# Chunked attention and a feed-forward layer on one core: smaller warming products, a held-back weight load and a new order of the first steps

## The chip, the cores and the metric

The kernel runs on one core of one Trainium2 chip. The metric is the device time of one execution in microseconds (us). The engines are TensorE (PE, matrix products; its weight loads are listed apart as PEld), VectorE (DVE), ScalarE (ACT), GpSimd (POOL) and SyncE (SP), whose queue issues the DMA transfers here.

## The reference

```python
chunk, scale = 64, 1 / np.sqrt(64)                   # q, k, v: [8, 8, 576, 64] float32
q_c, k_c, v_c = (a.reshape(8, 8, 9, 64, 64) for a in (q, k, v))
scores = scale * np.matmul(q_c, k_c.transpose(0, 1, 2, 4, 3))
scores = scores - np.max(scores, axis=-1, keepdims=True)
attn = np.exp(scores)
attn = attn / (np.sum(attn, axis=-1, keepdims=True) + 1e-09)
out = np.matmul(attn, v_c)
x = out.transpose(0, 2, 1, 3).reshape(4608, 512)
h = x @ w_in                                         # [512, 2048] float64
g = h * (1 / (1 + np.exp(-1.702 * h)))
return (g @ w_out).astype(np.float32)                # [2048, 512] float64
```

## The kernel before

The 4608 tokens are worked in nine blocks of 512. For each block the attention gives x, transposed, as a high and a low part (`x_h`, `x_l`); the first layer makes 16 groups of 128 hidden columns (`h_j`: three products of 512 columns for each of four slices of 128 dimensions, high by high, low by high, high by low); the gate gives `g_h` and `g_l`; the second layer adds them up in four PSUM tiles `po0` to `po3` (`o_j_t`). The weights arrive as float64 words. For group j (or for its halves j_0, the column part of w_in, and j_1, the row part of w_out, with j = 0 and 1), `raw` loads them, `wsc` and `wlow` (ACT), `wshift` and `wj` (DVE) turn the words into float32, and `wh` (ACT) and `w` (DVE) split that into two parts.

The change works on the start, in which nothing can be multiplied yet. The attention of the first block is done by `plan_first(u)` in four groups u = 0 to 3, each of two heads with 512 tokens. The steps of a group, with their engines: `q_u`, `k_u`, `v_u` (SP: loads, 256 KB each, into tiles `first_a` and `first_b`), `tqp_u` and `tkp_u` (PE: transposes by products with the identity; for u = 0 and 2 as 16 products of 64 by 64 each, L541, for u = 1 and 3 as 8 of 128 by 64 each, L549), `tq_u` and `tk_u` (ACT, for u = 1 `tk_u` on DVE: copies out of PSUM, L561 to L570), `s_u` (PE: 16 score products, L579), `m_u` and `sm_u` (DVE: maximum L584, subtraction L588), `ex_u` (ACT: exponential, L591), `z_u` (DVE: sum L595, plus 1e-9 L596, reciprocal L598), `n_u` (POOL: multiplication, L601), `ep_u` (PE: four transposes, L606), `et_u` (ACT: copy, L613), `xp_u` (PE: 16 products with v, L628), `xh_u` (ACT, L636) and `xl_u` (DVE, L640). A float32 product that isn't a transpose by the hardware's own mode is two loads and two products in the trace.

Before the first transposes, PE multiplies the identity by itself (`keep_warm`, L1720); nothing reads the result. A tile of the constant 1e-9 (`eps`) is set at the start.

What stands when is set by a table: `ORDER` is one string with the names of all 2754 steps, and `Plan.emit` runs the steps in that order, so that each engine gets its instructions in the order of the names; an engine works strictly in its own order and waits by semaphores. A DMA semaphore can be used again only when its last transfer has landed, so that SP has at most eight loads under way.

```python
plan.add(DMA, (n, 1.5, 384), at - 5.5, load, need=slot_users(j), make=e("raw"), take=[tag])
plan.add(PE, 3.4, -1000, lambda: keep_warm(ps_o, "po3", WARM), make="warm")
```

Of the kernel before, what the change touches and what calls it, by code (L numbers as in the profile page):

```python
# [237 lines left out]
def tile_chunk_attention_ffn(  # L238
# [20 lines left out]
    NTL = NT // P  # L259
    NB = NTL // TB  # L260
    BT = TB * P
    SCALE = 1.0 / float(D) ** 0.5
    NPE = 6
    NTMP = 3
    WARM = 7
    FILL = ()
    NH = 2
    RANKS = (-1.0, 9.0, 14.0, 20.0, 21.5, 31.0, 35.0, 37.5, 45.5, 52.0, 62.0, 70.0, 76.0, 82.5, 92.5, 100.0)
    K_ACT = (0, 2, 3)
    LOW_DVE = ()  # L270
    LEAD = 25
# [1514 lines left out]
```

## Time and profile before

| | |
|---|---|
| median of 3 runs | 813.99 us (812.33 to 816.24) |
| profiled execution, own time | 814.22 us |
| its span in the profile | 812.4 us |
| PE busy in the span | 803.3 us (99%) |
| DVE, ACT, POOL busy | 595.0, 380.3, 90.0 us |
| first stretch of PE without gaps begins | about 25.5 us |

The span runs from the first instruction to the last one; the execution's own time is 1.8 us longer. A PE that is shown as busy is not PE at its peak, since products are pipelined and their ends are modelled. Times below are counted from the start of the span.

### The profile page before, as it was taken

How to read it: one execution, taken by the hardware profiler on the slowest of the kernel's cores; microseconds unless marked ns; L12 is line 12 of the kernel's file. 1: busy time of each engine (PE TensorE's matmuls, PEld its weight loads, DVE VectorE, ACT ScalarE, POOL GpSimd, SP SyncE). 2: the span in 40 equal slices, each digit the busy share in tenths (PEclk: the TensorE clock that was granted, in tenths of full speed). 3: DMA queues.
4: the chain of work that ended last, by engine and by line, in shares of the span. 5: the costliest groups of instructions: out<-in, count | busy, mean ns of one | idle time of the engine just before them, and what ended most of it. 6: DMA issues, size and time to landing. Idle time of an engine off the chain costs nothing.

```text
span 812.4 us, 15467 instructions
## 1 busy us (share of the span) xinstructions
PE 803.3 (99%) x5934; PEld 666.6 (82%) x5934; DVE 595.0 (73%) x900; ACT 380.3 (47%) x610; POOL 90.0 (11%) x83
## 2 busy tenths in 40 slices
PE   7999999999999999999999999999999999999998
PEld 6788888888888888888888888888888888888887
DVE  4888974646567979886787888876878545659965
ACT  5998934334445546413345451523554512338450
POOL 1100004030045651000000010000001000000000
PEclk9999999999999999999999999999999999999999
DMA  9995646642366677667664538676533046766433
GB/s 266 301 349 127 160 94 182 166 97 52 66 186 169 172 198 215 179 184 216 180 159 130 133 80 217 178 215 192 156 118 105 0 128 193 230 202 220 134 100 105
DMA packets 240106, 133.17 MB, mean 164 GB/s; under 512 B 179104, under 2 KB 207776, under 8 KB 240032
## 3 DMA queue, kind: packets, MB, share of 16 engines
q1 hardware_dynamic: 240032, 132.18, 58.0%
q8 instruction: 47, 0.77, 0.4%
q14 instruction: 27, 0.22, 0.1%
HBM read 97.52 MB, written 32.51 MB: 160 GB/s over the span
## 4 chain that ended last, share of the span: by engine, by line
PE 97%; DMA 1%; ACT 0%; issue 0%; DVE 0%; SPq 0%; DVEq 0%
PE po L1643 13%; PE po L1645 13%; PE po L1644 13%; PE hp L867 9%; PE hp L869 9%; PE hp L868 9%; PE hp L1607 5%; PE hp L1609 5%; PE hp L1608 5%; PE acc_A L1133 3%; PE acc_B L1133 3%; PE s L1387 2%; PE x L1461 2%; PE acc_A L1126 2%; PE acc_B L1126 1%; DMA first_a<-in_k_dram 1%
## 5 line engine op out<-in xcount | busy, mean ns | idle before, releaser
L1643 PE MATMUL po<-w,g_l 128*128 128x512 f32 x448 | 176.4, 394 | 0.0
L1645 PE MATMUL po<-w,g_h 128*128 128x512 f32 x448 | 174.5, 390 | 0.0
L1644 PE MATMUL po<-w,g_h 128*128 128x512 f32 x448 | 174.5, 389 | 0.0
L1643 PEld LDWEIGHTS po<-w,g_l 128*128 128x128 f32 x448 | 84.1, 188 | 18.4 <-DVE g_l L918 0.4
L1645 PEld LDWEIGHTS po<-w,g_h 128*128 128x128 f32 x448 | 84.1, 188 | 17.6
L1644 PEld LDWEIGHTS po<-w,g_h 128*128 128x128 f32 x448 | 84.1, 188 | 16.9
L867 PE MATMUL hp<-w,w 128*128 128x512 f32 x224 | 87.5, 390 | 0.1
L869 PE MATMUL hp<-w,w 128*128 128x512 f32 x224 | 87.2, 389 | 0.0
L868 PE MATMUL hp<-w,w 128*128 128x512 f32 x224 | 87.2, 389 | 0.0
L1436 DVE STREAM_TRANSPOSE eT<-e 32x512 f32<-32x512 f32 x120 | 84.2, 702 | 3.1 <-POOL e L1417 1.2
L1417 POOL TENSOR_TENSOR e<-e,r 128x1024 f32<-128x1024 f32 x16 | 31.5, 1968 | 436.4 <-DVE r L1414 338.9
L1607 PE MATMUL hp<-x_l,w 128*128 128x512 f32 x184 | 72.1, 392 | 0.0
L1608 PE MATMUL hp<-x_h,w 128*128 128x512 f32 x184 | 71.6, 389 | 0.0
L1609 PE MATMUL hp<-x_h,w 128*128 128x512 f32 x184 | 71.6, 389 | 0.0
L1628 ACT ACTIVATE hp<-hp 128x512 f32<-128x512 f32 x48 | 28.0, 584 | 81.6 <-PE hp L1609 71.5
L1633 DVE TENSOR_TENSOR g_l<-hp,g_h 128x512 fp32r<-128x512 f32 x48 | 33.0, 688 | 44.9 <-ACT g_h L1629 44.6
L867 PEld LDWEIGHTS hp<-w,w 128*128 128x128 f32 x224 | 42.1, 188 | 9.9 <-issue 0.5
L869 PEld LDWEIGHTS hp<-w,w 128*128 128x128 f32 x224 | 42.0, 188 | 8.7
L868 PEld LDWEIGHTS hp<-w,w 128*128 128x128 f32 x224 | 42.0, 188 | 8.6
L867 PE MATMUL hp<-w,pieces 128*128 128x512 f32 x112 | 43.7, 390 | 0.0
L869 PE MATMUL hp<-w,pieces 128*128 128x512 f32 x112 | 43.6, 389 | 0.0
L868 PE MATMUL hp<-w,pieces 128*128 128x512 f32 x112 | 43.6, 389 | 0.0
(225 smaller groups left out, 1473.3 us busy)
## 6 DMA issues: line engine op xcount, KB each, us to landing
w<-seven SPq DMA_DIRECT2D x112, 256.0 KB, 3.1
pieces<-seven SPq DMA_DIRECT2D x56, 256.0 KB, 3.2
seven<-w SPq DMA_DIRECT2D x24, 512.0 KB, 3.7
raw<-in_moe_w_in_dram SPq DMA_DIRECT2D x16, 512.0 KB, 7.2
raw<-in_moe_w_out_dram SPq DMA_DIRECT2D x16, 512.0 KB, 6.9
four<-four_w SPq DMA_DIRECT2D x32, 256.0 KB, 3.5
raw<-in_q_dram SPq DMA_DIRECT2D x208, 32.0 KB, 2.2
raw<-in_k_dram SPq DMA_DIRECT2D x208, 32.0 KB, 2.2
```

The costliest lines, as they stand in the source:

```text
L867: nc.tensor.matmul(hp, w[:, 0, c], xl[:, c], start=c == 0, stop=False)
L868: nc.tensor.matmul(hp, w[:, 0, c], xh[:, c], start=False, stop=False)
L869: nc.tensor.matmul(hp, w[:, 1, c], xh[:, c], start=False, stop=c == 1)
L1133: nc.tensor.matmul(halves(o), gh[:, c], w, start=first, stop=stop, skip_group_check=not fresh)
L1436: nc.vector.transpose(st["et"][po : po + 32, :, 32 * a : 32 * a + 32], st["e"][pi : pi + 32, :, 32 * b : 32 * b + 32],)
L1607: nc.tensor.matmul(hp, wh, xl, start=cc == 0, stop=False)
L1608: nc.tensor.matmul(hp, wh, xh, start=False, stop=False)
L1609: nc.tensor.matmul(hp, wl, xh, start=False, stop=cc == NCC - 1)
L1633: nc.vector.tensor_tensor(gl, h_t[g], gh.bitcast(F32), op=ALU.subtract)
L1643: nc.tensor.matmul(po, gl[:, c], w[:, 0, :], start=first, stop=False)
L1644: nc.tensor.matmul(po, gh[:, c], w[:, 0, :], start=False, stop=False)
L1645: nc.tensor.matmul(po, gh[:, c], w[:, 1, :], start=False, stop=last)
```

## The change

Four things change. The warming is 14 products of 64 columns (`CH`) in place of 7 of 128. A small tile `hold` in the place of the first weight part (tag `w1a`) gets a quarter of the identity, and the last transpose product of `tkp_0` reads it there, so that the load `raw_1_0` into that place comes only after `tkp_0`. The 1e-9 is kept as a second row beside the sum, and both are added by a second sum over two elements in place of an addition. And `ORDER` is new from its first step to its last. After the first ten groups the product steps stand nearly where they stood.

```diff
-    "warm q_0 tqp_0 k_0 k_1 q_1 tkp_0 raw_1_0 tkp_1 tq_0 q_2 tk_0 tqp_1 k_2 xa_1 k_3 s_0 q_3 tq_1 tk_1 raw_2 "
...
-    WARM = 7
+    WARM = 14
...
-    eps = pad.tile([P, 96], F32, tag="pad", name="eps")[:, :16]
+    small = pad.tile([P, 96], F32, tag="pad", name="small")
+    eps = small[:, :16]
+    zeps = small[:, 32:64].rearrange("p (r c) -> p r c", r=2)
...
-    nc.vector.memset(eps, 1e-9)
+    nc.vector.memset(small, 1e-9)
+    hold = const.tile([P, 1024], F32, tag="w1a", name="hold")[:, :CH]
+    nc.vector.tensor_copy(hold[CH:], ident[CH:, CH:])
...
-            plan.add(DMA, (n, 1.5, 384), at - 5.5, load, need=slot_users(j), make=e("raw"), take=[tag])
+            plan.add(DMA, (n, 1.5, 384), at - 5.5, load, need=slot_users(j) + ["tkp_0"] * (name == "1_0"), make=e("raw"), take=[tag])
...
-                            nc.tensor.matmul(to, data, ident[r, r], start=True, stop=True)
+                            last = (u, i, t, h, half) == (0, 1, TB - 1, 1, 1)
+                            nc.tensor.matmul(to, data, hold[r] if last else ident[r, r], start=True, stop=True)
...
-            nc.vector.tensor_reduce(z, st["e"], axis=AX.X, op=ALU.add)
-            nc.vector.tensor_tensor(z, z, eps[:, :NK], op=ALU.add)
+            nc.vector.tensor_reduce(zeps[:, 0, :NK], st["e"], axis=AX.X, op=ALU.add)
+            nc.vector.tensor_reduce(z, zeps[:, :, :NK].rearrange("p r c -> p c r"), axis=AX.X, op=ALU.add)
...
-        warm = pool.tile([P, P], F32, tag=tag, name="warm")
+        warm = pool.tile([P, CH], F32, tag=tag, name="warm")
         for _ in range(count):
-            nc.tensor.matmul(warm, ident, ident, start=True, stop=True)
+            nc.tensor.matmul(warm, ident, ident[:, :CH], start=True, stop=True)
```

On PE, at the very start of the program, this stood before (a row is one or more products in a row; `qkTp` are the transposes, `s` the scores, `eTp` the transposed exponentials, the number behind the name is u):

```order
L1720 MATMUL warm_89<-ident_77 128x128 x7
L541 MATMUL qkTp_0_99<-ident_77,first_a_0_97 64x64 x32
L549 MATMUL qkTp_1_1_138<-ident_77,first_a_1_117 64x128 x8
L549 MATMUL qkTp_1_0_150<-ident_77,first_a_1_117 64x128 x8
L579 MATMUL s_0_164<-first_a_0_97 64x64 x16
L579 MATMUL s_1_190<-first_a_1_117 64x64 x16
L541 MATMUL qkTp_2_214<-ident_77,first_a_2_148 64x64 x32
L549 MATMUL qkTp_3_1_247<-ident_77,first_a_3_162 64x128 x8
L549 MATMUL qkTp_3_0_260<-ident_77,first_a_3_162 64x128 x8
L579 MATMUL s_2_287<-first_a_2_148 64x64 x16
L579 MATMUL s_3_311<-first_a_3_162 64x64 x16
L606 MATMUL eTp_0_330<-ident_77,first_b_0_210 128x128 x4
```

And this stands there now:

```order
L1726 MATMUL warm_93<-ident_77 128x64 x14
L547 MATMUL qkTp_0_111<-ident_77,first_a_0_91 64x64 x31
L547 MATMUL qkTp_0_111<-hold_83,first_a_0_91 64x64
L585 MATMUL s_0_148<-first_a_0_91 64x64 x16
L555 MATMUL qkTp_1_1_165<-ident_77,first_a_1_109 64x128 x8
L555 MATMUL qkTp_1_0_178<-ident_77,first_a_1_109 64x128 x8
L547 MATMUL qkTp_2_189<-ident_77,first_a_2_146 64x64 x32
L585 MATMUL s_1_235<-first_a_1_109 64x64 x16
L555 MATMUL qkTp_3_0_256<-ident_77,first_a_3_225 64x128 x8
L555 MATMUL qkTp_3_1_272<-ident_77,first_a_3_225 64x128 x8
L585 MATMUL s_2_287<-first_a_2_146 64x64 x16
L612 MATMUL eTp_0_309<-ident_77,first_b_0_176 128x128 x4
```

The scores of u=0 moved ahead of the transposes of u=1, those of u=1 behind the transposes of u=2, and the transposed exponentials of u=0 ahead of the scores of u=3.

On SP, the first loads before were these:

```order
L507 DMA first_a_1_117<-in_q_dram 128x2x256
L373 DMA raw_1_0_136<-in_moe_w_in_dram 128x4x128
L507 DMA first_a_2_148<-in_q_dram 128x2x256
L507 DMA first_a_2_148<-in_k_dram 128x2x256
L507 DMA first_a_3_162<-in_k_dram 128x2x256
L507 DMA first_a_3_162<-in_q_dram 128x2x256
L373 DMA raw_2_184<-in_moe_w_in_dram 128x4x128
L378 DMA raw_2_184<-in_moe_w_out_dram 128x512
L528 DMA first_b_0_210<-in_v_dram 128x4x64 x2
```

And these are they now:

```order
L512 DMA first_a_1_109<-in_q_dram 128x2x256
L512 DMA first_a_2_146<-in_q_dram 128x2x256
L512 DMA first_a_2_146<-in_k_dram 128x2x256
L378 DMA raw_1_0_223<-in_moe_w_in_dram 128x4x128
L512 DMA first_a_3_225<-in_q_dram 128x2x256
L512 DMA first_a_3_225<-in_k_dram 128x2x256
L378 DMA raw_0_0_254<-in_moe_w_in_dram 128x4x128
L383 DMA raw_0_1_270<-in_moe_w_out_dram 128x512
L533 DMA first_b_0_176<-in_v_dram 128x4x64 x2
```

The first weight part moved behind q and k of u=2 and waits there for PE, and the two parts of group 0 took the place of group 2 ahead of v.

On ACT the load of the gate's table, before just ahead of the first gate, now stands between the high parts of x of u=1 and the copy of the transposed exponentials of u=2 (a step `gt` with a one-element activation).

## Rows read from the trace of the kernel before

**Rows 1.** The page: busy us, share, instructions; then queue, packets, MB, share.

```profile
PE 803.3 (99%) x5934; PEld 666.6 (82%) x5934; DVE 595.0 (73%) x900; ACT 380.3 (47%) x610; POOL 90.0 (11%) x83
...
q8 instruction: 47, 0.77, 0.4%
```

**Rows 2.** Busy time by stage: window, length, each engine's us, clock, DMA share, GB/s.

```profile
1.36:4.65 3.29, 3.29 (x15) 3.06 (x15) 0.00 (x0) 0.66 (x1) 0.00 (x0) 1.00 0.76 236
4.65:11.67 7.02, 6.02 (x209) 5.62 (x209) 2.28 (x5) 2.73 (x4) 0.00 (x0) 1.00 1.02 329
...
13.65:25.50 11.85, 10.49 (x228) 8.11 (x227) 9.63 (x23) 10.54 (x19) 4.17 (x4) 1.00 0.96 257
25.50:800.00 774.50, 774.26 (x5425) 641.59 (x5426) 575.81 (x858) 365.15 (x586) 85.11 (x73) 1.00 0.58 161
...
809.00:812.40 3.40, 0.26 (x3) 0.05 (x1) 0.42 (x1) 0.00 (x0) 0.00 (x0) 1.00 0.33 116
```

**Rows 3.** The chain that ended last: start, us, what.

```profile
11.67 1.98 issue
```

**Rows 4.** DMA queues in 0 to 11.15 us, then in 11.2 to 12.2 us.

```profile
DMA packets 2949, 2.87 MB, mean 258 GB/s; under 512 B 142, under 2 KB 2949, under 8 KB 2949
...
q1 hardware_dynamic: 2949, 2.87, 81.1%
...
q8 instruction: 1, 0.02, 5.8%
```

**Rows 5.** Groups of PE's instructions, 1 to 5.5 us: count, busy us, mean ns, idle.

```profile
L1720 PE MATMUL warm<-ident 128*128 128x128 f32 x14 | 3.4, 433 | 1.4 <-POOL ident masks.py:199 1.4
...
L1720 PEld LDWEIGHTS warm<-ident 128*128 128x128 f32 x14 | 3.1, 330 | 1.4 <-POOL ident masks.py:199 1.4
```

**Rows 6.** Instructions in order of time, 4 to 14 us: start, us, what.

```profile
6.07 1.02 ACT L561 ACTIVATE first_a<-qkTp 128x1024 f32<-128x1024 f32 x1 [4.05 <-PE qkTp L541]
6.99 1.97 PE L549 MATMUL qkTp<-ident,first_a 128*64 128x128 f32 x32 [1.00 <-DMA first_a<-in_k_dram]
8.89 2.02 PE L579 MATMUL s<-first_a 64*64 64x64 f32 x61
11.74 0.63 ACT L591 ACTIVATE first_b<-first_b 128x512 f32<-128x512 f32 x1 [1.02 <-DVE first_b L588]
13.65 0.46 PE L541 MATMUL qkTp<-ident,first_a 64*64 64x64 f32 x16 [1.98 <-issue]
13.65 0.32 PEld L541 LDWEIGHTS qkTp<-ident,first_a 64*64 64x64 f32 x15 [2.07 <-issue]
```

**Rows 7.** DMA issues of 2.76 and 3.82 us: count, KB, us to landing.

```profile
raw<-in_moe_w_in_dram SPq DMA_DIRECT2D x1, 512.0 KB, 6.2
first_a<-in_k_dram SPq DMA_DIRECT2D x1, 256.0 KB, 6.5
```

**Rows 8.** Line L596, the addition of 1e-9: ns min/median/max, first and last start.

```profile
L596 DVE TENSOR_TENSOR z<-z,eps x4: 166/168/331, 14.1 to 22.3; 128x8 f32<-128x8 f32 x4
```

**Rows 9.** Instructions in order of time, 15 to 26 us.

```profile
15.74 0.69 DVE L595 TENSOR_REDUCE z<-first_b 128x8 f32<-128x512 f32 x1 [1.21 <-ACT first_b L591]
17.01 1.04 POOL L601 TENSOR_TENSOR first_b<-first_b,r 128x512 f32<-128x512 f32 x1 [1.28 <-DVE r L598]
17.13 0.69 DVE L584 TENSOR_REDUCE m<-s 128x8 f32<-128x512 f32 x1 [0.27 <-PE s L579]
17.86 0.69 DVE L588 TENSOR_TENSOR first_b<-s,m 128x512 f32<-128x512 f32 x1
18.27 1.09 PE L606 MATMUL eTp<-ident,first_b 128*128 128x128 f32 x8
23.58 0.19 PEld L1620 LDWEIGHTS hp<-x_l,w 128*128 128x128 f32 x1 [0.47 <-DVE x_l L640]
23.68 0.19 PEld L1621 LDWEIGHTS hp<-x_h,w 128*128 128x128 f32 x1
24.80 1.45 PE L628 MATMUL x<-first_b 64*64 64x64 f32 x64
```

350 rows, old and new, of the table ORDER are left out of this document.

## The prediction

> **What bounds the kernel now.** I read four views. The page first: TensorE (PE) has work in 99% of the span [rows 1], so time can only come from stretches in which PE stands. The windows by stage say where those are [rows 2]: from 25.5 to 800 us PE is busy 774.26 of 774.50 us, so the middle has nothing to give. After 809 us only the last store and the closing barrier are left (3.4 us), and the change does not touch them. What is left is the start: PE begins at 1.36, the first 3.29 us go to warming products that compute nothing, and of the 20.85 from 4.65 to 25.5 it is busy 6.02 + 10.49 = 16.51, so 4.3 us idle. Third, the chain of waits names the largest piece [rows 3]: 1.98 us of "issue" from 11.67 to 13.65, in which PE stands inside the transposes of group u=2 though nothing releases it. (The next largest is 1.00 before u=1's transposes, which wait for the second k [rows 6].) Fourth, the DMA queues show what that "issue" is [rows 4]: up to 11.15 us all 2949 packets belong to the data queue; the first packet of the queue "q8 instruction" lies in 11.2 to 12.2, and PE goes on 1.5 us after it. So PE had run out of instructions. The page gives 47 such packets for 2 x 5934 PE instructions, loads and products [rows 1], about 252 each.
>
> **The change part by part.**
>
> *Warming.* Now 14 loads and 14 products take 3.06 us, 0.219 each [rows 5]. PE passes 128 columns of f32 in 0.219 us here, but 16 pairs of them in 1.97 us of the transposes of u=1, 0.11 each with two at a time [rows 6]; the granted-clock row says 1.00 throughout [rows 2], but the pace is half, so I read the lower level, 1.2 GHz, for the warming. After the change there are 28 products of half the columns. If the columns set the pace, each takes 0.11 and the stretch stays 3.06 us. If the load of the 128-column weights sets it, each takes up to 0.219; at 4.65 us 13 would be left, 1.4 us if the clock then goes up as it does now, 2.9 us if it doesn't. The nearest row for a load alone is at 23.58: the next load starts 0.10 later [rows 9], under 0.11. I take 0, and keep 1.4 and 2.9 as upper ends. What it certainly adds is 28 instructions to PE's stream.
>
> *Instruction stall.* Before the stall PE ran 28 (warming) + 128 (u=0) + 64 (u=1) + 128 (s_0, s_1) + 97 of 128 (u=2; after the stall 16 products and 15 loads are left [rows 6]) = 445 instructions. With 28 more in front, the 445th is the fifth of s_1, since the new order has 56 + 128 + 64 + 64 + 128 = 440 before it. So the stall moves out of the transposes of u=2 to the head of s_1. When it ends no row shows. If the packet is asked for when PE enters the block of 252 before, that is instruction 193: now 37 into the 64 of u=1, at 8.0 us [rows 6], and the stall ends 5.65 later. Afterwards it is the ninth of s_0, at 7.2 us, so the end is 12.85. The late bound is the old time, 13.65; the early bound is no stall, s_1 as soon as its operands are there (10.9, below). I take 12.85.
>
> The Trainium skill, page "Runtime: NRT & Kernel Launch", section "Instruction fetch mechanics", says that a block of 16 KiB (256 instructions) is fetched while the one before runs, so that crossing a boundary is "mostly hidden", and that PE holds 2048 instructions. The trace agrees on the block and disagrees on the rest: 1.98 us stood open at about instruction 445. By the page's rule nothing would stall after the change and the sum would be 811.6; by the row's stall it is 813.5.
>
> *First weight part held back.* k_2 is issued at 3.82 and lands 6.5 us later, at 10.3, behind a 512 KB weight load that was issued at 2.76 and lands at 2.76 + 6.2 = 9.0 [rows 7]; between the two lie q_2 and k_2, 512 KB as well. So 512 KB take about 1.3 us, and without the weight ahead of it k_2 comes at about 9.0, q_2 before it; the new PE order wants them at 9.9. The weight load waits on SP for the last product of u=0 (5.99), and q_3, k_3, two more weight parts and all v loads queue behind it. Up to 9.0 the data queue is full anyway, so the bytes lie back to back and the weight lands at about 10.4, q_3 and k_3, half as large, at 11.1 and 11.7. ACT's first pass over the weight comes at about 10.8 in the new order. I cost it at nothing; its cover is 0.4 us, and without it the price is the weight's 1.3 us on ACT at most.
>
> *1e-9 as a second row.* Four additions of 0.17 to 0.33 us [rows 8] become four sums over 16 numbers; nearest row the same one. Between 0 and 0.16 us each where POOL works beside; I take 0. The wider memset and the copy of `hold` run on DVE before PE's first transposes, where DVE has nothing to do up to 4.65 [rows 2]: 0.
>
> *Order.* Before, s_0 stands on PE behind the transposes of u=1, which wait for k_1 until 6.99, and starts at 8.89 [rows 6]. After, it needs only ACT's copy (6.07 + 1.02 [rows 6]): 7.15, done at 8.13 (half of the 2.02 of s_0 and s_1). u=1's transposes run 8.1 to 9.9 (1.97 less the last product's 0.2), u=2's to 10.85 (0.93, twice the 0.46 of the 16 products after the stall). s_1 waits for ACT's copy of u=1, and ACT does the exponential of u=0 first: 8.13 + 0.2 to the maximum, 0.73 to the subtraction, 0.72 to the exponential [rows 9], 0.5 to the copy behind it, 0.6 for that: 10.9. With the stall s_1 runs 12.85 to 13.8. From its end, maximum, subtraction, exponential, sum, reciprocal: 0.2 + 0.73 + 0.72 + 0.66 (0.63 [rows 6] and the handing over) + 1.27 (15.74 to 17.01 [rows 9]), so POOL starts u=1 at 17.4, ends 1.04 later, and PE's transposes of it start at 18.5. Now POOL starts at 17.01, but those transposes stand behind s_3 and the ones of u=0 (four of the eight from 18.27): 18.7. Gain 0.2. For u=2 and u=3: from 13.8 on PE does the transposes of u=3 (1.75), s_2 (1.0), the transposes of u=0's exponentials (0.44) and s_3 (1.0) to 18.0; now both are done only at 18.7. Here 0.7 is gained, and on DVE a weight subtraction (0.6) no longer stands between the last maximum and its subtraction. So the last x products, now 24.80 to 26.2 [rows 9], end about 0.9 earlier. Two products of the first layer (0.46) that now lie ahead of them come behind: net 0.45. The gelu table load (1.28) moves from just before the first gate to ACT's wait for u=2's exponentials; if that cover is gone it costs up to 1.28, and then the first gate has 1.28 less before it.
>
> *Sum.* Warming 0, hold 0, second row 0, order and stall -0.45, the rest 0: 814.2 - 0.45 = 813.8 against the profiled execution's own 814.22 (span 812.4 plus 1.8). That is 0.2 above the median of the runs, 813.99, so I forecast **813.5**.
>
> **The rivals.**
>
> *No stall, or a short one.* If the instructions are there, s_1 starts at 10.9 instead of 12.85, and all behind it moves: another 1.9 or so, 811.6. For it: the fifth instruction of s_1 is at the very edge, and the request lies only nine instructions into a step that waits; a request that runs ahead of that wait would go out at 5.7, 1.5 earlier. The page named above would have it so. Against: 3.2 us from request to packet in a full data queue now.
>
> *The stall ends when it did.* If the packet's time hangs on the data queue and not on the request, the end is 13.65, and the 0.8 is lost: 814.3, no change.
>
> *Slower: the warming gets longer.* If loads at the lower clock take twice the 0.10, they set the pace; transposes start 1.4 later and all behind them: 813.5 + 1.4 = 814.9. It decides from 0.5 us on. With the clock staying low, 2.9 and half-speed transposes: 816.5 to 817.
>
> *A new wait further on.* The order is rewritten up to the end; PE's 0.24 us idle in 774.5 could become a few us where a weight part or gate now comes late. Through the first weight groups the DMA order differs mainly in the second rows load, which now goes ahead of a weight load. Nothing speaks for a large one; 816 to 818.
>
> **How the numbers follow.** Forecast 0.35, stall end unchanged 0.15, no stall 0.2, longer warming 0.2, low clock or a new wait 0.1. The runs before spread from 812.33 to 816.24, and a median of such runs is uncertain by over 1 us. The range reaches from no stall less 0.7 (below it, 811.0) to the longer warming plus 1.3 (816.2); that leaves out about 2 in 10. A measurement can tell about 0.5%, 4.07 us, from no change; no case of gain reaches it, since of the 4.3 us of idle PE no more than 2.6 are won in any of them, and of the slow cases only the worst. So faster 0.03, same 0.93, slower 0.04.
>
> **What would show it.** Right: the "issue" gap lies between u=2's transposes and s_1 and ends near 12.9; the warming stretch still ends near 4.5; s_0 starts near 7.2; the PE stretch without gaps begins about half a us earlier; after it PE idles no more than now. Wrong: the first transposes start near 6 (warming longer), transposes run at half pace after 5 us (clock), ACT waits for the held weight, or idle PE appears after 26 us.

## The result and the profile after

The changed kernel takes 819.87 us (median of 6 runs, 818.87 to 821.27) where the kernel before takes 814.73 beside it (6 runs): by the ratio on record 1.0077 of it, 95% interval 1.0063 to 1.0091. That ratio stands for 6.3 us; the two medians differ by 5.1. Three of the six runs of the kernel before took over 815 us here, and in the later batches its median was 813.17 to 813.55. Shares of the loss below go by ratios. The profiled execution took 819.52 us, its span is 817.7. The page's row of engines, which answers to [rows 1]:

```profile
PE 808.9 (99%) x5948; PEld 671.8 (82%) x5948; DVE 595.8 (73%) x901; ACT 380.6 (47%) x610; POOL 90.1 (11%) x83
```

PE is busy 5.6 us longer with 14 more instructions of each kind. Busy time by stage, as [rows 2]:

```profile
1.36:7.53 6.17, 6.17 (x29) 6.05 (x29) 0.17 (x1) 0.66 (x1) 0.00 (x0) 1.00 0.82 246
7.53:15.00 7.47, 6.30 (x121) 6.00 (x122) 1.78 (x3) 1.65 (x2) 0.00 (x0) 1.00 0.56 184
15.00:28.50 13.50, 12.20 (x318) 9.87 (x314) 12.16 (x26) 12.40 (x23) 4.18 (x4) 1.00 0.96 278
28.50:800.00 771.50, 769.97 (x5398) 637.25 (x5399) 572.44 (x852) 365.24 (x585) 85.19 (x73) 1.00 0.58 161
```

The warming now fills 6.17 us. From 7.53 to 15.00 PE is busy for 6.30 us and starts only 121 products; in the same stretch the kernel before is busy for 5.49 us and starts 173:

```profile
7.53:15.00 7.47, 5.49 (x173) 5.16 (x170) 5.07 (x10) 3.17 (x5) 0.31 (x1) 1.00 1.07 342
```

Behind 28.5 us 1.5 us of idle PE stand where 0.24 stood from 25.5 us on [rows 2]. The granted-clock column is 1.00 in every stretch, as before, so it doesn't show the low clock at the start; the pace of like products does. PE's instructions in order of time (start, us, what), answering to [rows 5, 6]:

```profile
1.36 6.24 PE L1726 MATMUL warm<-ident 128*128 128x64 f32 x28 [1.36 <-POOL ident masks.py:199]
7.53 1.87 PE L547 MATMUL qkTp<-ident,first_a 64*64 64x64 f32 x59
...
10.69 1.97 PE L585 MATMUL s<-first_a 64*64 64x64 f32 x32 [1.17 <-ACT first_a L567]
12.59 3.09 PE L555 MATMUL qkTp<-ident,first_a 128*64 128x128 f32 x32
15.61 1.16 PE L547 MATMUL qkTp<-ident,first_a 64*64 64x64 f32 x64
```

and its loads there:

```profile
1.36 6.05 PEld L1726 LDWEIGHTS warm<-ident 128*128 128x128 f32 x28 [1.36 <-POOL ident masks.py:199]
```

Here lies the loss. 28 loads take 6.05 us, 0.216 each, as much as one took with 128 columns behind it [rows 5]: the load of 128 columns of weights sets the pace, and half the columns buy nothing. And after the warming the clock is still at its lower level (1.2 GHz, by the pace): s_0's 32 records take 1.97 us, where 61 records of s_0 and s_1 took 2.02 before [rows 6]; u=1's transposes take 3.09 where they took 1.97 [rows 6], and only inside them does the pace double, near 15 us. (All 32 at the low clock take 3.68, in a run below; so (3.09 - 1.97) / (3.68 - 1.97) = 65% of them were slow.) PE has no issue wait over 0.2 us: the stall of [rows 3] is gone.

The hold shows on SP's queue (start, us of issue, what):

```profile
3.28 0.47 SPq L512 DMA_DIRECT2D first_a<-in_k_dram  x1
9.60 0.37 SPq L378 DMA_DIRECT2D raw<-in_moe_w_in_dram  x1
```

For 5.85 us SP issues nothing. In the kernel before, SP went on issuing then, the second load of [rows 7] among others.

### The profile page after: what moved, and what is told of

Same layout as the page of the kernel before. It is cut to its first block, busy times and chain, and to the rows that moved or that the text cites. A ratio compares the mean times of both kernels' runs of the same rounds, so it can differ in the third digit from the quotient of the medians.

```text
span 817.7 us, 15491 instructions
## 1 busy us (share of the span) xinstructions
PE 808.9 (99%) x5948; PEld 671.8 (82%) x5948; DVE 595.8 (73%) x901; ACT 380.6 (47%) x610; POOL 90.1 (11%) x83
## 4 chain that ended last, share of the span: by engine, by line
PE 97%; ACT 1%; DMA 1%; issue 0%; SPq 0%; POOL 0%; DVE 0%; POOLq 0%
PE po L1649 13%; PE po L1651 12%; PE po L1650 12%; PE hp L873 9%; PE hp L875 9%; PE hp L874 9%; PE hp L1613 5%; PE hp L1614 5%; PE hp L1615 5%; PE acc_A L1139 3%; PE acc_B L1139 3%; PE s L1393 2%; PE x L1467 2%; PE acc_A L1132 2%; PE acc_B L1132 1%; PE warm L1726 1%
```

## The experiments

Theory: nearly all of the loss is the warming, by two things that belong together: the 128-column load sets its pace, and behind it the clock is still low. Rivals: the hold (an empty data queue), the new order, and 28 more instructions on PE. Every kernel was timed in turn with the kernel before; the ratio to it stands with its 95% interval. Fences of rows show PE's instructions in order of time, or its loads (PEld), unless the sentence ahead says otherwise.

### Undoing the warming, and the warming alone

**e1: the kernel after with the old warming.**

```diff
-    WARM = 14
+    WARM = 7
...
-            nc.tensor.matmul(warm, ident, ident[:, :CH], start=True, stop=True)
+            nc.tensor.matmul(warm, ident, ident, start=True, stop=True)
```

> The kernel after, with the warming of before again (7 products of 128 columns); hold, second row and order stay. Theory (the warming costs nearly all): PE's first transposes start at about 4.65 us instead of 7.53, the transposes of u=1 take about 2.0 us for 32 records instead of 3.1, and the time is 814.5 to 816, about 1 above before from the small waits after 300 us. Rival (the hold or the new order costs it): 818.5 to 820, PE waiting for first_a or raw early on.

814.78 us, 1.0016 [1.0006, 1.0025]. 0.61% of the 0.77% is gone. In its profile the transposes start at 4.64, but the clock rose late here too: s_0 has 1.97 us and u=1's transposes 2.50.

```profile
7.80 1.97 PE L585 MATMUL s<-first_a 64*64 64x64 f32 x32 [1.17 <-ACT first_a L567]
9.70 2.50 PE L555 MATMUL qkTp<-ident,first_a 128*64 128x128 f32 x32
```

**e2: the kernel before with the new warming alone** (the same lines the other way round).

> The kernel before with only the warming changed to 14 products of 64 columns. Theory (the 128-column weight load sets the pace, 0.21 us each, and the clock rises late): 28 records take about 6.0 us, first transposes start at about 7.5, 32 transposes of u=1 take about 3 us, time 818 to 820. Rival (hold or order): time within 1 us of before, 814 to 815.5.

819.16 us, 1.0061 [1.0043, 1.0079]: the same 0.61%. The transposes of u=1 run slow to the end here, 3.68 us for 32:

```profile
7.53 1.99 PE L541 MATMUL qkTp<-ident,first_a 64*64 64x64 f32 x64
9.44 3.68 PE L549 MATMUL qkTp<-ident,first_a 128*64 128x128 f32 x32
```

Theory and measurement agree from both sides, and with the short warming the hold and the order can have no more than the 0.16% that e1 leaves. That the two figures are equal is luck: the six runs of e2 spread from 815.63 to 819.96, and its profiled execution lost about a us again from 27 us on, where the clock fell (last section).

### Which property of the warming

**e17: the kernel after with narrow weights.** One edit: as many products, as many instructions and as many columns as in the kernel after, but 64 columns to load.

```diff
-        warm = pool.tile([P, CH], F32, tag=tag, name="warm")
+        warm = pool.tile([P, CH], F32, tag=tag, name="warm")[:CH]
...
-            nc.tensor.matmul(warm, ident, ident[:, :CH], start=True, stop=True)
+            nc.tensor.matmul(warm, ident[:, :CH], ident[:, :CH], start=True, stop=True)
```

> The kernel after with one edit: its 14 warming products take only 64 columns of the identity as weights too. Hold, second row and order stay, and PE gets as many instructions as in the kernel after. Theory (the 128-column load at the low clock is what the change lost by): a record takes 0.107 us, the 28 take 3.0 us, the transposes start near 4.6, and the time falls from 1.0077 of before to 1.001 to 1.003, as with the old warming. Rival (28 more instructions or the hold cost it): 1.006 and more.

814.6 us, 1.0018 [1.0008, 1.0027]: 0.59% back by this edit alone, as the theory had it, so neither the number of instructions nor the hold was what cost. Its loads and its transposes of u=2:

```profile
1.36 3.06 PEld L1726 LDWEIGHTS warm<-ident 128*64 128x64 f32 x28 [1.36 <-POOL ident masks.py:199]
...
10.59 1.16 PE L547 MATMUL qkTp<-ident,first_a 64*64 64x64 f32 x64
```

28 loads in 3.06 us, 0.109 each: half the width, half the time. The transposes of u=2 begin at 10.59, in the kernel after at 15.61: 5.02 us, of which 2.99 is the warming and the rest the half-speed products behind it. This execution gives back 1.1 us in an issue wait at 17 us that the kernel after doesn't have, and the two profiled times differ by 4.03:

```profile
18.35 0.33 PE L585 MATMUL s<-first_a 64*64 64x64 f32 x3 [1.09 <-issue]
```

**e6: the kernel before with 14 such narrow products** (the same edit, with WARM = 14).

> The kernel before with 14 warming products of 64 columns by weights of only 64 columns. If the width of the loaded weights sets the pace, a record takes 0.107 us instead of 0.213, the 28 records take 3.0 us and the transposes start near 4.6; if a load costs the same at any width, 6.05 us and 7.5. With the first, the columns stream all the time and the clock should rise as before: within 1 us of before.

814.42 us, 1.0011 [1.0001, 1.0022], transposes from 4.53 us: the narrow loads take 3.06 us here too.

**e4: the kernel before with 14 products of 128 columns.**

```diff
-    WARM = 7
+    WARM = 14
```

> The kernel before with 14 warming products of 128 columns instead of 7, so as many records as in the kernel after, but with the columns streaming all the time. If the late clock comes from the half-filled columns: the pace goes from 0.21 to 0.11 us a record at about 5.1 us, inside the warming, which ends near 6.2; the transposes of u=1 take about 2 us, and the time is 815.5 to 816.5. If it comes from anything else in the longer warming: the pace stays at 0.21 up to about 7.5, transposes run at half pace, 818 to 820.

815.97 us, 1.0032 [1.002, 1.0045], 2.6 us by the ratio: the longer warming with as many columns to multiply as to load. The clock rises inside it (28 loads take 5.70 us instead of 6.05), and all behind it runs at full pace:

```profile
7.18 1.16 PE L541 MATMUL qkTp<-ident,first_a 64*64 64x64 f32 x64
8.27 1.97 PE L549 MATMUL qkTp<-ident,first_a 128*64 128x128 f32 x32
```

The rest of e2's loss, 0.29%, goes with the late clock (and with the second fall in e2); that the 64 columns make the clock late rests on these profiles more than on the times, since the intervals of e2 and e4 touch.

**e5: the kernel before with 7 products of 64 columns**, the half columns without the length.

```diff
-            nc.tensor.matmul(warm, ident, ident, start=True, stop=True)
+            nc.tensor.matmul(warm, ident, ident[:, :CH], start=True, stop=True)
```

> The kernel before with 7 warming products of 64 columns: as many loads as before, half the columns. If the load sets the pace, the 14 records still take 3.06 us and the transposes start at 4.65. If the half-filled columns hold the clock back, these then run at half pace (u=0's 64 records in 1.9 us in place of 1.1) for some us and the time is 814.5 to 816; if only the length of the warming matters, the clock rises as before and the time is within 0.5 us of before.

814.37 us, 1.0007 [0.9996, 1.0018]: no difference that can be told. The warming still takes 3.06 us, and in this execution the clock came later, inside u=1's transposes:

```profile
4.54 1.99 PE L541 MATMUL qkTp<-ident,first_a 64*64 64x64 f32 x64
6.45 2.68 PE L549 MATMUL qkTp<-ident,first_a 128*64 128x128 f32 x32
...
12.08 0.46 PE L541 MATMUL qkTp<-ident,first_a 64*64 64x64 f32 x16 [0.24 <-issue]
```

What that costs seems hidden: the waits for k_1 and for instructions, 1.00 and 1.98 us [rows 6, 3], are 0 and 0.24 here. So 0.32% for the length and 0.07% for the columns don't add up to the 0.61% of both. That with both the slow products run on after this cover is used up is a reading of these profiles; no run shows it by itself.

**e18: the opposite warming**, 2 products of 448 columns on the kernel before.

```diff
-    WARM = 7
+    WARM = 2
...
+        many = ident[:, :CH].unsqueeze(1).broadcast_to([P, 7, CH])
...
-            nc.tensor.matmul(warm, ident, ident, start=True, stop=True)
+            nc.tensor.matmul(warm, ident, many, start=True, stop=True)
```

> The kernel before with the opposite warming: 2 products of 448 columns (the identity's first 64 columns seven times over) in place of 7 of 128. As many columns, 4 loads in place of 14, so the stretch stays near 3.0 us, and the 445th PE instruction comes 24 instructions further on, in the last tenth of u=2's transposes. Theory: columns that stream all the time raise the clock as before, so within 0.5 us of before. If it were the loads that raise the clock, the transposes would run at half pace and the time be 1 us or more above.

815.2 us, 1.0015 [1.0001, 1.0028], 1.2 us slower by the ratio, between the two expectations. The warming keeps its length (transposes from 4.65), the clock rose inside u=0's transposes (1.86 us), and the issue wait, now with 6 of u=2's 64 products left, is as long as ever:

```profile
13.38 0.34 PE L541 MATMUL qkTp<-ident,first_a 64*64 64x64 f32 x6 [2.01 <-issue]
```

Five of its 12 runs list a mean granted clock of 0.997 or 0.998 and take 815.2 to 816.95 us; the other seven have a median of 813.86, half a us above before. So about half of the 1.2 us goes with a clock that fell again (last section). The run doesn't decide between columns and loads; 20 instructions less ahead of the wait (not 24, as I had counted) win nothing.

### The hold, the second row and the order

**e3: the kernel after without the hold.**

```diff
-... need=slot_users(j) + ["tkp_0"] * (name == "1_0"), make=e("raw"), ...
+... need=slot_users(j), make=e("raw"), ...
...
-                            nc.tensor.matmul(to, data, hold[r] if last else ident[r, r], start=True, stop=True)
+                            nc.tensor.matmul(to, data, ident[r, r], start=True, stop=True)
```

> The kernel after without the hold: raw_1_0 is issued without waiting for tkp_0; warming, second row and order stay. Theory: the warming stays the cost, 819 to 820, at most 1 us below the kernel after, with the data queue full between 9 and 12.5 us where it is empty now. Rival (the hold costs it): 815 to 816.

818.47 us, 1.0064 [1.0051, 1.0077], 0.13% below the kernel after with overlapping intervals. From 5 to 10 us the DMA engines are busy 0.98 of the time, with the hold 0.45 (by the windows); it hardly matters.

**e7: order and second row alone** (e1 and e3 together), and **e8: the order alone**, with the addition of 1e-9 as before:

```diff
-            nc.vector.tensor_reduce(zeps[:, 0, :NK], st["e"], axis=AX.X, op=ALU.add)
-            nc.vector.tensor_reduce(z, zeps[:, :, :NK].rearrange("p r c -> p c r"), axis=AX.X, op=ALU.add)
+            nc.vector.tensor_reduce(z, st["e"], axis=AX.X, op=ALU.add)
+            nc.vector.tensor_tensor(z, z, eps[:, :NK], op=ALU.add)
```

> The kernel after with the warming of before and without the hold: order and second row are left. With the hold worth about 1 us, as it was under the long warming (818.47 on a chip where before took 813.17, 0.13% below the kernel after by ratio), this stands 0.5 to 1.2 us below the kernel with the hold, at 813.2 to 814.3. If the hold is free with the short warming, it stays at 814.8.

> The new order alone: 7 warming products of 128 columns, no hold, 1e-9 by an addition. Theory: the second row costs under 0.3 us, so the same as the run with order and second row, 813.2 to 814.3. Rival (the four second sums are slower than the additions and stand in the chain): 0.5 us or more below it.

e7 814.85 us, 1.0019 [1.001, 1.0029]; e8 814.78, 1.0017 [1.0008, 1.0025]. With the short warming no cost of the hold can be told (1.0016 with it in e1), against my expectation, and none of the second row. What is left of the loss, 0.17%, belongs to the order. In both the stall is back at full length. The chain of e7 (start, us, what), as [rows 3], with lines left out:

```profile
7.24 1.15 PE s L582 x32
...
11.38 0.47 PE s L582 x16
11.85 1.90 issue
13.74 0.68 PE s L582 x15
...
15.49 0.60 ACT first_a L567
...
17.09 0.56 ACT raw L392
17.66 0.55 ACT raw L385
...
22.34 1.28 ACT L1732
23.64 0.20 ACT gelu L1732
...
24.91 0.47 ACT first_b L616
25.38 0.04 issue
25.43 0.69 PE x L631 x32
```

From 15.49 to 25.38 the chain never leaves ACT. So I suspected the load of the gate's table (1.28 + 0.20 us) and moved it.

**e9, e10, e11: the table load behind the first gate again**, in e8, in e1 and in the kernel after. In the order's table:

```diff
-... hh_1_0 wshift_0_0 hh_1_1 ep_2 gt xl_1 et_2 ...
+... hh_1_0 wshift_0_0 hh_1_1 ep_2 xl_1 et_2 ...
-... w_0_1 raw_3 wh_2 wsc_1_1 gl_0 w_2 ...
+... w_0_1 raw_3 wh_2 wsc_1_1 gl_0 gt w_2 ...
```

> The new order alone (as in the run of the order alone, 814.78 where before took 813.31), with one step moved: the load of the gate's table stands behind the first gate again, where before has it, and not ahead of ACT's copy of u=2's transposed exponentials. Theory (the order's 0.17% is this table load, 1.28 + 0.20 us in the middle of a run of ACT work without gaps from 15.5 to 25.4): 813.2 to 813.9, equal to before within 0.5 us. Rival (the order costs elsewhere): 814.6 to 815.

> The kernel after with the warming of before and the table load behind the first gate; hold, second row and the rest of the order stay. Theory (table load on ACT's path): 1.0 to 1.5 below the same kernel with the early table load (814.78 where before took 813.17), so 813.2 to 813.9. If moreover the hold gives PE's instruction block a free data queue, PE shows no issue gap of over 0.3 us at about the 445th instruction, where the order alone had 1.9 to 2.0, and the time could fall below before, to 812.5.

> The kernel after with only the table load moved behind the first gate. Theory: the two causes add, so 1.0 to 1.5 us are won of the kernel after's 0.77%, and 0.58 to 0.65% are left for the long warming (ratio to before 1.0058 to 1.0065). Rival (with the long warming PE waits for something else, and the table load is hidden): 1.0070 to 1.0080.

815.68 us, 1.0026 [1.0016, 1.0037]; 816.93, 1.0041 [1.0029, 1.0054]; 820.19, 1.0082 [1.0068, 1.0096]. None is faster than with the early load: they are 0.09, 0.25 and 0.05% above it, the middle one alone clear of the intervals. That theory, which expected 1.0 us less or more, falls. With the late load PE waits for the first gate instead (e10):

```profile
33.62 0.47 PE L1649 MATMUL po<-w,g_l 128*128 128x512 f32 x1 [0.67 <-DVE g_l L1639]
```

**e12 and e16: three more warming products in the gap ahead of s_0**, in e10 and in e1.

```diff
-    FILL = ()
+    FILL = (3,)
```

> As the run with the warming of before and the late table load, with three more warming products of 128 columns between the transposes of u=0 and s_0, where PE stood 1.4 us. They take 0.65 us at the high clock and 1.3 us at the low one, and fit into the gap. If that gap is what kept the clock low in the kernel with the short warming and the hold (pace 0.21 us up to 11 us), the transposes of u=1 now take 1.97 us and the time is 0.5 to 1 us lower. Rival (the clock's rise does not hang on this gap): the same time within 0.4 us.

> The kernel after with the warming of before, and three more warming products of 128 columns in the gap before s_0; hold, second row, order with its early table load stay. The late table load cost 0.9 us in the kernel that had the same fill and 816.19, so 815.0 to 815.5 by that alone. If the fill wins the 0.7 us between 816.93 and 816.19 here too, 814.0 to 814.4, below the same kernel without fill (814.78) and still not below before.

816.19 us, 1.0034 [1.0021, 1.0046], and 815.87, 1.0024 [1.0012, 1.0037]: 0.07% below e10, 0.08% above e1, both within the intervals, and e16 above both of its expectations. No gain of a filled gap can be told.

**e13 and e14: half of the new order.** e13 has the new order up to the first gate's low part (`gl_0`) and the old one from there; e14 the other way round. All else as before. In effect, with `that start` for the names already placed:

```diff
-ORDER = old
+ORDER = new[: new.index("gl_0") + 1] + [n for n in old if n not in that start]    # e13
+ORDER = old[: old.index("gl_0") + 1] + [n for n in new if n not in that start]    # e14
```

> The order alone, cut in two: the new order up to the first gate (its first 118 or so steps, early table load), then the old order for all that is left; warming, loads and the addition as before. If the order's 0.17% arises in the start, 814.5 to 815 (0.15% above before); if it arises in what follows, within 0.5 us of before.

> The other half: the old order up to the first gate, then the new order. If the order's 0.17% arises in the start, within 0.5 us of before; if in what follows, 0.15% above it.

816.28 us, 1.003 [1.0017, 1.0042], and 815.74, 1.002 [1.0007, 1.0034]. Both are slower than before, and neither is faster than the whole new order: where start and rest don't fit there are waits of their own (in e14 PE waits 1.26 us before 32.14 us for a weight part from ACT), so this doesn't locate the 0.17%.

**e15: the kernel before, unchanged**, a second profile.

> The kernel before once more, unchanged, for a second profile of it. If the moment at which TensorE's clock rises and the length of the wait for instructions differ from one execution to the next, its time of 1.98 us for the issue gap and the rise at about 5 us come out otherwise here, by several tenths of a us; if they belong to the program, they are the same within 0.1 us.

813.07 us, span 811.3, against 814.22 and 812.4 of the first profile.

```profile
4.54 1.16 PE L541 MATMUL qkTp<-ident,first_a 64*64 64x64 f32 x64
12.56 0.46 PE L541 MATMUL qkTp<-ident,first_a 64*64 64x64 f32 x16 [1.19 <-issue]
```

The wait for instructions is 1.19 us here and 1.98 there [rows 3], at the same instruction (16 products left, as in [rows 6]). The clock is up when the transposes start: 1.16 us for all 64. Both differ from one execution to the next, as the second expectation had it.

## Why the prediction was wrong

Forecast 813.5, no change, range 811.0 to 816.2; measured 819.87 and slower by 0.77%. By its own steps:

| step | predicted | measured |
|---|---|---|
| warming | 0 | 0.61% (e1, e2), 0.59% (e17): some 5.0 us |
| hold | 0 | 0.13% with overlapping intervals under the long warming (e3), none to tell under the short (e1 against e7) |
| second row | 0 | none to tell (e7 against e8) |
| order, the stall's end in it | -0.45 us | 0.16 to 0.19% (e1, e7, e8, e17): some 1.4 us slower |

0.61 and 0.17 make 0.78, the whole of the 0.77, each with an uncertainty of 0.1 to 0.2.

**The step that failed is the price of the load.** The prediction read the lower clock out of the pace of the warming, and a few sentences later priced the warming's load by the row at 23.58, 0.10 us [rows 9], which is at full clock; so it took the warming at 0 and left the longer warming to a rival. At the lower clock that row means 0.20, and 0.216 was measured. Then 28 records take 6.05 us, and "the columns set the pace" was wrong from the first record. The rows for it were there: 28 times twice 0.10 is 5.6. The Trainium skill, page "TensorE: Matmul & The Clock Gate", section "LDWEIGHTS (loading the stationary operand)", states a time by the number of weight columns alone, P / 1.2 ns, which makes an estimate of 107 ns for 128. The runs agree that the columns of the weights set it (0.216 and 0.109 us for 128 and 64, the kernel after and e17) and disagree with one figure for both clocks (0.10 us for 128 at the higher one, the row at 23.58).

**Its second half was named and under-priced.** The rival "with the clock staying low" gave 2.9 us and 816.5 to 817. The mechanism happened: the transposes start 2.88 us later (7.53 against 4.65) and the products behind them run slow. That second part was taken as 0.1 to 0.6 us. It was 2.0 to the start of u=2's transposes (5.02 less 2.99, the kernel after against e17), because the low clock lasted to near 15 us. The chance on it and on new waits together was 0.1.

**The stall.** The count was right: in e7, with 28 instructions less, it stands behind s_1's 16th product, at 28 + 128 + 64 + 64 + 128 + 32 = 444 instructions. It ended at 13.74, not at 12.85: the rival "the stall ends when it did". In the changed kernel PE comes to that instruction only near 16.6 us, at the head of s_1, and has it by then; so the stall vanishes and pays back a part of the loss. Coming late is not the only way: e17 is at the same count at 11.6 us and doesn't wait there either.

**The order.** The start of s_0 was right as to the mechanism (7.15 predicted, 7.24 in e7 with the early clock). Of the gain of 0.9 at the last x products 0.1 is there: they end at 26.12 us in e7 (25.43 + 0.69) and at 26.25 before (24.80 + 1.45 [rows 9]). Nearly all of the rest is the stall's end, 0.89 later than taken; the prediction's own rival priced that at 0.8. From the end of s_1 to that of the last x products it reckoned 11.5 us, and e7 takes 11.7 (14.42 to 26.12). It followed that path along DVE and POOL and left out that the new order gives ACT a queue without a hole, by the chain of e7 from 15.49 to 25.38 us, with five passes over weights (2.78 us by its rows) and the table load among the attention's copies. That this makes the order slower is not shown: by this reckoning it comes to 0.2 us in e7 and 0.5 in e8 (14.66 to 26.65), and the one piece that I moved made it no faster.

The profile on which the gain was worked out had a stall of 1.98 us, the other profile of the same kernel 1.19: up to 0.8 of the idle time that the order was to win is not there in every execution. Here lies a rival that no run tests: with like stalls, 1.98 and 1.90 us, the profiled executions of before and e7 have the same span, 812.4, so the order's cost may be that its wait is the long one more often (1.82 to 2.15 us in e7, e8, e9, e10 and e13; 0.24 to 2.01 in before, e4, e5, e6, e14, e15 and e18). Against it speak e1, which has no such wait and 0.16%, and e16 with 0.63 us and 0.24%. Where the 0.17% arises stays open.

**New waits further on.** The 1.5 us of idle PE behind 28.5 us are no work of the order: most are waits for DMA near 365 and 740 us, and e2 and e4, which keep the old order, have such waits of 1.0 and of 0.8 + 0.2 us. What brings them about is not shown.

No version tried beats the kernel before. Of the four edits none gains, and the warming makes most of the loss.

## What to carry to other kernels

A duration is good only at the clock at which its row was taken: where the pace of like instructions shows TensorE at half speed, double the prices that come from rows at full speed before using them. In the shapes run here, at the lower clock, a product cost the longer of its weight load and its columns: 0.219 us with 128 columns of weights and 128 to multiply, 0.216 with 128 and 64, 0.109 with 64 and 64. So cutting the columns below the width of the weights bought nothing, and e17 shows that cutting both does. And one profile's idle time is one execution's: before a gain of a us is worked out from a stall, see in a second profile whether it is there.

## What the runs showed of the hardware

- PE's wait for instructions stands at the same count whatever the instructions are: with 16 products left in u=2's transposes (before, e5, e15), behind s_1's 16th product (e7), with 6 left in e18 (8 + 128 + 64 + 128 + 116 = 444). Its length does not: 0.24, 1.19, 1.98 and 2.01 us in e5, e15, before and e18, and none at that count in e1, e2, e17 and the kernel after. A second such wait stands behind the 698th instruction, 254 further on: 1.09 us in e17 and 1.36 in e6.
- The moment at which TensorE's clock goes from 1.2 to 2.4 GHz differs between executions of one kernel: by the pace of u=0's 64 transposes, ahead of them in e15 (1.16 us for all), and inside them in the first profile of before (1.34 us). e1 and e10 differ only in where the table load stands, further on, and in e1 it rose near 11 us, inside u=1's transposes, in e10 ahead of s_0, which takes 1.15 us where it took 1.97 in e1:

```profile
4.65 1.34 PE L541 MATMUL qkTp<-ident,first_a 64*64 64x64 f32 x64
...
7.80 1.15 PE L585 MATMUL s<-first_a 64*64 64x64 f32 x32 [1.17 <-ACT first_a L567]
```

(The first row is of before, the second of e10.) The Trainium skill, page "TensorE: Matmul & The Clock Gate", says in its section "What's actually happening" that the moment varies from run to run, by 500 ns either way. The first pair agrees; e1 and e10 lie 3 us or more apart, which is more than that. Behind warmings of as many columns to multiply as to load it came between 4 and 8 us in most profiles and near 11 in e1; behind those of 64 columns on 128-column loads, at 8 us (e5) and between 13 and about 15 (e2, e3, e11, the kernel after).
- It can fall again: in e2 the granted clock is 0.61 in the four us below (window, length, each engine's us, clock, DMA share, GB/s), behind two waits of PE of 0.59 and 0.58 us, and in e6 0.50 from 20 to 26 us, behind a wait of 1.36. The first window is of e2, the second of e6:

```profile
26.00:30.00 4.00, 3.77 (x73) 2.87 (x71) 3.83 (x7) 2.76 (x6) 1.04 (x1) 0.61 1.03 370
...
20.00:26.00 6.00, 5.95 (x80) 4.45 (x76) 4.90 (x13) 4.95 (x11) 2.08 (x2) 0.50 0.97 274
```

- It goes with the time of a run: of the 122 runs of the kernel before beside the experiments, 7 list a mean granted clock of 0.997 or 0.998 and take 814.73 to 815.75 us; the other 115 have a median of 813.31.
